# Where the numerator of a rational activation is kept in the first half of a fused attention and two-MoE kernel

## The chip, the core and the metric

The kernel runs on one core of a Trainium2 chip. Its engines are TensorE (PE, with its weight loads shown apart as PEld), VectorE (DVE), ScalarE (ACT), GpSimd (POOL) and SyncE (SP), which only issues transfers. Each engine works through its own queue in order. The metric is the time of one execution on the device in microseconds. Before the change it is 1502.45 us, the median of three runs from 1498.46 to 1506.28.

## What is computed

Three layers in a row: an attention whose keys and values are averaged over groups of eight, a dense layer pair with a rational function between its two products, and a routed layer with eight experts. The change lies in the middle one:

```
h = x @ w_in                                  # 4608 x 512 by 512 x 2048
P = a0 + a1*h + a2*h^2 + a3*h^3
Q = 1 + |b0|*|h| + |b1|*h^2
g = P / (Q + 1e-6)
y = g @ w_out                                 # 2048 x 512
```

The output of the middle layer is routed (each token to one of eight experts by the sorted scores, 576 tokens each) and goes through a two-layer expert. All products are made of rounded parts: an operand is split into a high part and a remainder, and three products (high by high, high by remainder, remainder by high) are summed in PSUM.

## The kernel before

The 4608 tokens are cut into 18 blocks of 256. The 2048 columns of the middle layer are done in two halves of 1024: for all blocks the first half, with its partial outputs stored, then for all blocks the second half. Attention is interleaved with the first half, since it makes the `x` of each block. After the second half come the routing and the experts. In the trace the first half ends at about 596 us, the second at about 1000 us.

A half of a block (or of a pair of blocks) consists of steps. There are 72 steps in each half. A step multiplies `x` by 256 columns of `w_in` (or 128 columns for a pair of blocks) into one PSUM bank `ph` of 128 x 512 numbers (`mm_h`, line L701), and then makes `g` from it:

- `act1`: ACT makes |h| into `ms` (L716), a2 + a3*h into `mw` (L717) and |b0| + |b1|*|h| into `mq` (L719). DVE multiplies `mw` by h (L721), and then makes the numerator without its constant, (mw + a1)*h, which it writes **back into the bank `ph`** (L722). The product `mq*ms` is a `tt` operation (L353), which POOL does.
- `act2`: ACT makes 1/Q in `mr` by a logarithm and an exponential (L734, L736). DVE makes the high part `hi` = (numerator + a0)*`mr` (L737), then `t` = Q*`hi` (L739) and the difference `t` = numerator + a0 - `t` (L741). POOL multiplies it by `mr`, which is the remainder `lo` (L353). `hi` and `lo` together are a buffer `mg` or `mgx`.
- `mm_y`: PE multiplies `hi` by both parts of `w_out` (L805, L806) and `lo` by its high part (L803), into two further banks of 260 columns per 128 tokens, which stay in use over the steps of a block.

In the first half a bank `ph` is thus in use from the step's first matmul to L741. PSUM has eight such banks, named `pa0` to `pa7`. They are shared with the scores (L560), the transposes (L595) and the products (L613 to L616) of attention, and with the preparation of weights (L418 to L422, L440, L444). `mw` and `mq` are rings of three buffers each, taken by the step's number, so a buffer is written again three steps later. `mr` has two and `mt` three.

The order on each engine is not written by hand. Each operation is recorded with its engine, an assumed duration, what it reads and what it writes. A list scheduler then runs through the whole program in its own assumed time: at each point it takes the ready operation with the lowest number on an engine, and an operation that needs a new bank (`Dyn` of `cls_a`) waits until one is free. The instructions are issued in the order that results, and the banks are handed out by it too. The assumed duration of a DVE operation with two tensors depends on its size alone. Before 105 us the scheduler also puts matmuls of zeros on PE (L339) where it expects PE to be idle for 0.4 us or more.

Of the kernel before, what the change touches and what calls it, by code (L numbers as in the profile page):

```python
# [18 lines left out]
ALU = mybir.AluOpType  # L19
# [4 lines left out]
B, H, S, D = 8, 8, 576, 64  # L24
# [7 lines left out]
NB = NT // BLK  # L32
# [97 lines left out]
class Order:  # L130
# [18 lines left out]
    def op(self, eng, dur, fn, r=(), w=(), prio=None, nbytes=0, late=0.0):  # L149
        o = Op()  # L150
        o.alts, o.start, o.late = None, None, late
        o.eng, o.dur, o.fn, o.succ, o.npred, o.ready, o.nbytes = eng, dur, fn, [], 0, 0.0, nbytes
        o.idx = len(self.ops)
        o.prio = o.idx - self.ahead if prio is None else prio
        o.alloc, o.uses, o.bank = [], [], None
        preds = set()
        for k in r:
            p = self.lastw.get(k)
            if p is not None:
                preds.add(p)  # L160
        for k in w:
            p = self.lastw.get(k)
            if p is not None:
                preds.add(p)
            preds.update(self.readers.get(k, ()))
        for k in r:
            self.readers.setdefault(k, []).append(o)
        for k in w:
            self.lastw[k] = o
            self.readers[k] = []  # L170
        for k in {id(x): x for x in (*r, *w)}.values():
            d = k[0] if isinstance(k, tuple) else k
            if isinstance(d, Dyn) and d not in o.uses:
                if d.refs == 0:
                    o.alloc.append(d)
                    o.bank = d
                d.refs += 1
                o.uses.append(d)
        preds.discard(o)
        o.npred = len(preds)  # L180
        for p in preds:
            p.succ.append(o)
        self.ops.append(o)
        return o
# [98 lines left out]
def c_tt(n):  # L283
    return 0.067 + 0.00104 * n


def c_stt(n):
    return 0.06 + 0.00118 * n
# [10 lines left out]
class Kern:  # L299
# [408 lines left out]
    def act1(self, st):  # L708

        nc, op, i = self.nc, self.op, st["i"]  # L710
        ph = st["ph"]
        hk = [(ph, 0)]
        w, q, s = self.mw[i % 3], self.mq[i % 3], self.ms[i % 2]
        st["w"], st["q"] = ph, q
        N = 2 * BLK
        op("Act", c_act(N), lambda: nc.scalar.activation(s(), ph(), AF.Abs), r=hk, w=[s])  # L716
        op("Act", c_act(N, 0, 2), lambda: nc.scalar.activation(w(), ph(), AF.Identity, scale=self.a3(), bias=self.a2()),  # L717
           r=hk + self.sk, w=[w])
        op("Act", c_act(N, 1, 2), lambda: nc.scalar.activation(q(), s(), AF.Identity, scale=self.b1a(), bias=self.b0a()),  # L719
           r=[s] + self.sk, w=[q])  # L720
        op("DVE", c_tt(N), lambda: nc.vector.tensor_tensor(w(), w(), ph(), op=ALU.mult), r=hk, w=[w])  # L721
        op("DVE", c_stt(N), lambda: nc.vector.scalar_tensor_tensor(  # L722
            ph(), w(), self.a1(), ph(), op0=ALU.add, op1=ALU.mult), r=[w], w=hk)
        self.tt(N, q, q, s, ALU.mult, r=[s], w=[q])

    def act2(self, st):

        nc, op, i = self.nc, self.op, st["i"]
        w, q, r, t = st["w"], st["q"], self.mr[i % len(self.mr)], self.mt[i % MTB]
        hi, lo = g = self.mgl.pop(0)  # L730
        self.mgl.append(g)
        st["hi"], st["lo"] = hi, lo
        N = 2 * BLK
        op("Act", c_act(N, 1, 1), lambda: nc.scalar.activation(r(), q(), AF.Ln, scale=2.0 ** -LNS, bias=self.qcs()),  # L734
           r=[q], w=[r])
        op("Act", c_act(N, 1, 1), lambda: nc.scalar.activation(r(), r(), AF.Exp, scale=-1.0, bias=self.nls()), w=[r])  # L736
        op("DVE", c_stt(N), lambda: nc.vector.scalar_tensor_tensor(hi(), w(), self.a0(), r(), op0=ALU.add, op1=ALU.mult),  # L737
           r=[(w, 0), r], w=[hi])
        op("DVE", c_stt(N), lambda: nc.vector.scalar_tensor_tensor(t(), q(), self.qc(), hi(), op0=ALU.add, op1=ALU.mult),  # L739
           r=[q, hi], w=[t])  # L740
        op("DVE", c_stt(N), lambda: nc.vector.scalar_tensor_tensor(  # L741
            t(), w(), self.a0(), t(), op0=ALU.add, op1=ALU.subtract), r=[(w, 0), self.hring(st)], w=[t])
        self.tt(N, lo, t, r, ALU.mult, r=[t, r], w=[lo])

    def late(self, st):
# [755 lines left out]
    def route(self, k):  # L1501

        nc, V, rop = self.nc, self.nc.vector, self.rop
        D = lambda dur, fn, r=(), w=(), late=False: rop("DVE", dur, fn, r=r, w=w, late=late)
        L = lambda dur, fn, r=(), w=(): D(dur, fn, r, w, k > 0)
        tt, ts, stt = V.tensor_tensor, V.tensor_scalar, V.scalar_tensor_tensor
# [9 lines left out]
        q = lambda i: self.q8()[:, i, :]  # L1516
        z = lambda i: self.z1()[:, i:i + 1]
        qk, zk = (lambda i: (self.q8, i)), (lambda i: (self.z1, i))
        K, BQ, ch, M, S2 = self.K, self.BQ, self.ch, self.M if k else self.Mb, self.S2
        cq, cid, ra = self.cq, self.cid, self.ra  # L1520
        rk = lambda x: (self.rp, id(x))
        kk = lambda t, *a: [(t, n) for n in range(*(a or (NB,)))]
        c8 = (ch, 8)
# [28 lines left out]
        def ahead():  # L1552
            cw = lambda t, a, z: t().rearrange("p (g t) -> p g t", t=4)[:, a:z]
            wb = lambda n: self.wrb().unsqueeze(1).unsqueeze(3).to_broadcast([128, n, E, 4])
            for a, z, key in ((0, 8, rk(ch)), (8, 9, c8)):
                if a:
                    D(.1, lambda: ts(ch()[:, 8], self.R()[:, 8], 8.0, None, op0=ALU.is_equal), r=kk(self.R, NB - 2, NB), w=[c8])
                else:
                    D(.34, lambda: V.tensor_reduce(cq()[:, 0:8], K[0]().rearrange("p e g t -> p g t e"), op=ALU.max, axis=AX.X), r=[K[0]], w=[(cq, 0)])
                    own(a, z, key)  # L1560
# [16 lines left out]
        if not last:  # L1577
            if k == 0:
                J, jk = self.small(501, 5)
                D(.07, lambda: V.tensor_copy(J(), self.c("J")), r=[self.rc, *kk(self.R, NB - 2)], w=[jk])  # L1580
                D(.43, lambda: ts(ch()[:, 0:8], self.R()[:, 0:8], 8.0, None, op0=ALU.is_equal), r=kk(self.R, NB - 2), w=[rk(ch)])
                D(.06, lambda: V.memset(self.open8(), 1.0), r=[jk], w=[rk(self.open8)])
            spread(self.kq, BQ)

            def rest():
# [15 lines left out]
              r=[self.rc, (self.thr, 0)], w=[(T, 0), self.rj])  # L1601
            D(.15, lambda: ts(T()[:, E:2 * E], self.c("sel"), so(0)(), None, op0=ALU.mult, op1=ALU.add, accum_out=self.rj()),
              r=[self.rc, (self.sole, 0)], w=[(T, 1), self.rj])
            rop("PE", .2, lambda: nc.tensor.matmul(pt()[:, 0:2 * E], self.c("ones"), T(), start=True, stop=True),
                r=[(T, 0), (T, 1), self.rc], w=[pt])
# [5 lines left out]
              r=[(self.sole, 1), (self.sole, 2)], w=[self.flag])  # L1611
# [5 lines left out]
            def settle():  # L1617
# [4 lines left out]
              w=[rk(M), zk(2), qk(2), K[0], rk(K[1]), K[2], BQ, self.cc, self.chw, (self.chw, 0), (self.chw, 8), self.ge, self.cand, self.nn, self.njunk, self.X, (self.rp, 496), (self.rp, 8), (self.thr, 0), *self.BJ, *[(self.cnt, j) for j in range(4)]])  # L1622
# [361 lines left out]
```

## Time and profile before

| | |
|---|---|
| median of three runs | 1502.45 us (1498.46 to 1506.28) |
| the profiled execution | 1500.95 us, of which the span from the first to the last instruction is 1499.2 us |
| PE busy | 1451.5 us, 97% of the span |
| PEld, DVE, ACT, POOL busy | 87%, 72%, 61%, 58% |
| first half without its first 60 us (60 to 596 us) | PE 518.0, DVE 417.8, ACT 421.2, POOL 361.2 of 536 us |

A busy PE is not PE at its peak, since the ends of matmuls are modelled. But where the profile shows PE idle, time is lost unless PE makes it up from work that is ready, and nothing else in this program is as full as PE. What a stretch has to give is therefore read from PE's idle time in it, from what ended that idle time, and from the granted clock, which falls in some places after PE has been idle. In the list of waits, "PE pa L560 <- DVE mt L741" means that line L560 of PE waited, and that the instruction of line L741 on DVE came last before it went on.

### The profile page before, as it was taken

Reading aid. Unit: us, or ns where it says so; the run is one execution under the profiler, and the core shown is the slowest. Engines: PE = TensorE matmul, PEld = TensorE weight load, DVE = VectorE, ACT = ScalarE, POOL = GpSimd, SP = SyncE. Lnnn points to the kernel's source line nnn. Section 1 sums busy time; section 2 is a strip of 40 time slices with the busy share of each in tenths; the row PEclk is TensorE's granted clock in tenths of the full one; section 3 lists DMA queues with packets and bytes.
Section 4 is the critical chain, followed back from the end, with each engine's and each line's share of the span. In section 5 each row is a group of like instructions: output and inputs, shape, how many; then the busy total and the mean of one; then the engine's idle time right before and its main releaser. Section 6 shows DMA issues by size and latency. Waiting matters only on the chain. (4 is left out here: it accounts for less than half of the span.)

```text
span 1499.2 us, 27379 instructions
## 1 busy us (share of the span) xinstructions
PE 1451.5 (97%) x9516; PEld 1311.2 (87%) x9516; DVE 1077.9 (72%) x2909; ACT 917.9 (61%) x2203; POOL 877.0 (58%) x809
## 2 busy tenths in 40 slices
PE   8899999999999999999999999998999999999998
PEld 7899978888998999888999899766988988988997
DVE  6898787858678587897777877987878877831220
ACT  5887886868778686765446655842554543542431
POOL 5877887557666465764456554842465654653621
PEclk9999999999999999999999999999899999999999
DMA  6672543232422354531343333013254433433400
GB/s 218 221 238 99 168 144 131 80 113 89 144 99 71 103 153 126 166 82 63 111 113 85 85 97 102 1 47 126 86 173 141 152 113 118 155 121 99 140 26 32
DMA packets 109686, 173.62 MB, mean 116 GB/s; under 512 B 10336, under 2 KB 74208, under 8 KB 109536
## 3 DMA queue, kind: packets, MB, share of 16 engines
q1 hardware_dynamic: 84640, 134.02, 27.7%
q0 software_dynamic: 24896, 37.76, 9.1%
q8 instruction: 75, 1.23, 0.3%
q14 instruction: 75, 0.61, 0.1%
HBM read 122.29 MB, written 49.46 MB: 115 GB/s over the span
## 5 line engine op out<-in xcount | busy, mean ns | idle before, releaser
L701 PE MATMUL pa<-xh,wih 128*128 128x256 f32 (+1 forms) x576 | 202.3, 351 | 2.7 <-ACT ex L573 1.2
L701 PE MATMUL pa<-xh,wil 128*128 128x256 f32 (+1 forms) x576 | 195.4, 339 | 0.2 <-POOL wil L353 0.2
L701 PE MATMUL pa<-xl,wih 128*128 128x256 f32 (+1 forms) x576 | 195.2, 339 | 0.0
L353 POOL TENSOR_TENSOR mwq<-mwq,ms 128x512 f32<-128x512 f32 x96 | 130.2, 1357 | 97.4 <-ACT mwq L719 95.9
L716 ACT ACTIVATE ms<-pa 128x512 f32<-128x512 f32 x144 | 85.9, 596 | 113.0 <-PE pa L701 102.0
L1820 PE MATMUL pa<-yth,w1h 128*128 128x256 f32 (+1 forms) x512 | 146.0, 301 | 0.9 <-issue 0.7
L1820 PE MATMUL pa<-ytl,w1h 128*128 128x256 f32 (+1 forms) x512 | 144.9, 299 | 0.0
L1820 PE MATMUL pa<-yth,w1l 128*128 128x256 f32 (+1 forms) x512 | 144.8, 298 | 0.0
L353 POOL TENSOR_TENSOR mg<-mt,mr 128x512 fp32r<-128x512 f32 x75 | 96.9, 1292 | 61.1 <-DVE mt L741 43.2
L805 PE MATMUL pa<-woh,mg 128*128 128x260 f32 x480 | 125.5, 287 | 4.3 <-DVE mg L737 1.9
L806 PE MATMUL pa<-wol,mg 128*128 128x260 f32 x480 | 123.9, 284 | 0.0
L1873 POOL DMA_INDIRECT out<-ob,ix x40 | 39.0, 976 | 144.0 <-ACT ob L1869 116.0
L701 PEld LDWEIGHTS pa<-xh,wih 128*128 128x128 f32 x576 | 109.8, 191 | 14.5 <-ACT ex L573 2.0
L701 PEld LDWEIGHTS pa<-xh,wil 128*128 128x128 f32 x576 | 109.3, 190 | 13.1 <-POOL wil L353 0.4
L701 PEld LDWEIGHTS pa<-xl,wih 128*128 128x128 f32 x576 | 109.7, 190 | 9.1
L573 ACT ACTIVATE ex<-pa,nm 128x72 f32<-128x72 f32 (+2 forms) x320 | 98.6, 326 | 19.8 <-DVE nm L564 14.3
L741 DVE SCALAR_TENSOR_TENSOR mt<-pa,scal,mt 128x512 f32<-128x512 f32 x144 | 106.9, 743 | 1.3
L1823 ACT ACTIVATE h2h<-pa 128x256 fp32r<-128x256 f32 (+1 forms) x128 | 51.0, 407 | 84.9 <-PE pa L1820 79.5
L1854 PE MATMUL pa<-w2h,h2h 128*128 128x512 f32 x256 | 102.7, 401 | 0.0
L1854 PE MATMUL pa<-w2h,h2l 128*128 128x512 f32 x256 | 100.1, 391 | 0.0
L1828 DVE SCALAR_TENSOR_TENSOR h2l<-pa,h2h 128x256 fp32r<-128x256 f32 x128 | 53.7, 419 | 63.9 <-ACT h2h L1823 59.1
L1820 PEld LDWEIGHTS pa<-yth,w1h 128*128 128x128 f32 x512 | 95.9, 192 | 2.1 <-issue 1.5
(438 smaller groups left out, 4942.4 us busy)
## 6 DMA issues: line engine op xcount, KB each, us to landing
mwq<-in_w SPq DMA_DIRECT2D x42, 512.0 KB, 4.4
wraw<-in_w SPq DMA_DIRECT2D x22, 512.0 KB, 5.0
ya_d<-ya SPq DMA_DIRECT2D x18, 520.0 KB, 2.8
yab<-ya_d SPq DMA_DIRECT2D x18, 520.0 KB
kvraw<-in_kT SPq DMA_DIRECT2D x16, 576.0 KB, 4.2
x_d<-xh SPq DMA_DIRECT2D x18, 512.0 KB, 3.9
x_d<-xl SPq DMA_DIRECT2D x18, 512.0 KB
xh<-x_d POOLq DMA_DIRECT2D x18, 512.0 KB
```

The source lines that it names most:

```text
L353: self.g.either({"Pool": (p_tt(n), lambda: nc.gpsimd.tensor_tensor(out(), x(), y(), op=alu)), "DVE": (c_tt(n), lambda: nc.vector.tensor_te ...
L573: op("Act", c_act(NK, 0, 1, 1), lambda h=h: nc.scalar.activation(e()[:n, h, :], sv()[:, h, :], AF.Exp, bias=nm()[:n, h:h + 1], accum_out=s ...
L701: nc.tensor.matmul(o, w()[:, c, f], x()[:, c].rearrange("p b t -> p (b t)") if two else x()[:, c, :], start=c == 0 and k == 0, stop=c == 3 ...
L716: op("Act", c_act(N), lambda: nc.scalar.activation(s(), ph(), AF.Abs), r=hk, w=[s])
L741: op("DVE", c_stt(N), lambda: nc.vector.scalar_tensor_tensor(t(), w(), self.a0(), t(), op0=ALU.add, op1=ALU.subtract), r=[(w, 0), self.hri ...
L805: nc.tensor.matmul(o, hi()[:, f], w(woh), start=first, stop=False)
L806: nc.tensor.matmul(o, hi()[:, f], w(wol), start=False, stop=False)
L1820: nc.tensor.matmul(ps()[:, 0:n], w()[:, c, fs], x()[:, c, :], start=i == 0, stop=i == 11)
L1823: fop("Act", c_act(n), lambda hh=hh, t=t, n=n, ps=ps: nc.scalar.activation(hh()[:, t], ps()[:, 0:n], AF.Relu), r=[ps], w=[(hh, half)])
L1828: fop("DVE", c_stt(t1 - t0), lambda hh=hh, o=o, o0=o0, ps=ps, t0=t0, t1=t1, half=half: nc.vector.scalar_tensor_tensor(o()[:, o0:o0 + t1 - ...
L1854: nc.tensor.matmul(ps(), x()[:, t], w()[:, f % 2, :], start=f == 0 and i == 0, stop=False)
L1873: fop("Pool", 1.05, lambda ob=ob, c=c, n=n: nc.gpsimd.indirect_dma_start(out=self.out, out_offset=bass.IndirectOffsetOnAxis(ap=ix()[:n, c: ...
```

## The change

In the first half L722 writes the numerator into `mw`, its own SBUF input, in place of the bank. The bank `ph` is therefore read last by L722. L737 and the difference (L741 before) read the numerator from `mw`. The product Q*`hi` is written into a fresh PSUM bank `tp` in place of `mt`. The difference reads it there, and writes `mt`. The second half is computed as before. Two further lines add dependencies in the routing, so that operations which write into one bank there keep their order. In the changed kernel the lines of `act2` are called L740 (before L737), L743 (L739) and L745 (L741), and those of `mm_y` L807, L809 and L810 (L803, L805 and L806).

```diff
@@ act1
         op("DVE", c_stt(N), lambda: nc.vector.scalar_tensor_tensor(
-            ph(), w(), self.a1(), ph(), op0=ALU.add, op1=ALU.mult), r=[w], w=hk)
+            (ph if st["half"] else w)(), w(), self.a1(), ph(), op0=ALU.add, op1=ALU.mult),
+           r=[w] if st["half"] else hk, w=hk if st["half"] else [w])
+        if st["half"] == 0:
+            st["w"] = w
@@ act2
         op("DVE", c_stt(N), lambda: nc.vector.scalar_tensor_tensor(hi(), w(), self.a0(), r(), op0=ALU.add, op1=ALU.mult),
-           r=[(w, 0), r], w=[hi])
-        op("DVE", c_stt(N), lambda: nc.vector.scalar_tensor_tensor(t(), q(), self.qc(), hi(), op0=ALU.add, op1=ALU.mult),
-           r=[q, hi], w=[t])
+           r=[(w, 0), w, r], w=[hi])
+        tp = t if st["half"] else Dyn(self.cls_a)
+        op("DVE", c_stt(N), lambda: nc.vector.scalar_tensor_tensor(tp(), q(), self.qc(), hi(), op0=ALU.add, op1=ALU.mult),
+           r=[q, hi], w=[tp])
         op("DVE", c_stt(N), lambda: nc.vector.scalar_tensor_tensor(
-            t(), w(), self.a0(), t(), op0=ALU.add, op1=ALU.subtract), r=[(w, 0), self.hring(st)], w=[t])
+            t(), w(), self.a0(), tp(), op0=ALU.add, op1=ALU.subtract), r=[(w, 0), w, tp, self.hring(st)], w=[t])
@@ route, ahead()
-                    D(.1, lambda: ts(ch()[:, 8], self.R()[:, 8], 8.0, None, op0=ALU.is_equal), r=kk(self.R, NB - 2, NB), w=[c8])
+                    D(.1, lambda: ts(ch()[:, 8], self.R()[:, 8], 8.0, None, op0=ALU.is_equal), r=[(self.rp, 501), *kk(self.R, NB - 2, NB)], w=[c8])
@@ route
-                D(.43, lambda: ts(ch()[:, 0:8], self.R()[:, 0:8], 8.0, None, op0=ALU.is_equal), r=kk(self.R, NB - 2), w=[rk(ch)])
+                D(.43, lambda: ts(ch()[:, 0:8], self.R()[:, 0:8], 8.0, None, op0=ALU.is_equal), r=[jk, *kk(self.R, NB - 2)], w=[rk(ch)])
```

No instruction is added to DVE, ACT or POOL. The rows of PE of the two kernels differ all through the first half. Behind it they are the same apart from the banks they name and from small groups, at the seam between the halves and in the routing, which stand some rows earlier or later. PE's matmuls of zeros (L339) are 212 before and 225 after.

On PE, at about 237 to 243 us of the trace, near the end of block 1's steps (`mg1` and `mg2` are the buffers of two steps, `pa` the banks, `en` the attention weights), before:

```order
L560 MATMUL pa4_231<-kbd0_100,qraw0_102 128x144 x2
L595 MATMUL pa5_233<-ident_115,en2_436 128x128 x3
L803 MATMUL pa3_197<-woh2_1169,mg1_979 128x260
L803 MATMUL pa0_130<-woh2_1169,mg1_979 128x260
L805 MATMUL pa3_197<-woh3_1593,mg2_1159 128x260
...
L805 MATMUL pa1_148<-woh3_1593,mg2_1159 128x260
L806 MATMUL pa1_148<-wol3_1605,mg2_1159 128x260
L701 MATMUL pa6_270<-xh1_795,wih0_145 128x512
```

and in the changed kernel at the same place:

```order
L560 MATMUL pa7_274<-kbd0_100,qraw0_102 128x144 x2
L595 MATMUL pa0_130<-ident_115,en2_436 128x128 x3
L701 MATMUL pa5_233<-xh1_795,wih0_145 128x512
L701 MATMUL pa5_233<-xl1_813,wih0_145 128x512
L701 MATMUL pa5_233<-xh1_795,wil0_191 128x512
L701 MATMUL pa5_233<-xh1_795,wih0_145 128x512
L701 MATMUL pa5_233<-xl1_813,wih0_145 128x512
L701 MATMUL pa5_233<-xh1_795,wil0_191 128x512
L807 MATMUL pa3_197<-woh2_1251,mg1_1080 128x260
```

Six matmuls of a coming step have moved ahead of the products with `lo` of `mg1` (L803, now L807).

On PE, at about 341 to 348 us of the trace, two steps of the same weights `wih2` apart, before (the products with `hi` of `mg0` are the L805 rows, the eight rows of attention's L613 to L616 are cut to the first):

```order
L560 MATMUL pa3_197<-kbd1_112,qraw1_104 128x144 x2
L613 MATMUL pa1_148<-pth0_285,vmh0_120 128x192
...
L803 MATMUL pa4_231<-woh1_628,mg4_1458 128x260
L803 MATMUL pa5_233<-woh1_628,mg4_1458 128x260
L805 MATMUL pa4_231<-woh1_628,mg0_865 128x260
...
L595 MATMUL pa1_148<-ident_115,en2_436 128x128 x3
L701 MATMUL pa0_130<-xh0_353,wih2_976 128x512
```

and in the changed kernel, where the left-out rows ahead of L809 hold eight of attention, two L807, one L595 and nine more L701:

```order
L560 MATMUL pa7_274<-kbd1_112,qraw1_104 128x144 x2
L701 MATMUL pa1_148<-xh0_353,wih2_1014 128x512
L701 MATMUL pa1_148<-xl0_362,wih2_1014 128x512
L701 MATMUL pa1_148<-xh0_353,wil2_1023 128x512
L613 MATMUL pa5_233<-pth0_285,vmh0_120 128x192
...
L809 MATMUL pa0_130<-woh1_628,mg0_873 128x260
```

All twelve matmuls of the next step have moved ahead of the products with `hi` of `mg0`.

On DVE, at one step of the first half (`mg0` is its high part), before:

```order
L737 SCALAR_TENSOR_TENSOR mg0_865<-pa6_270,scal_93,mr1_932 128x512
L627 SCALAR_TENSOR_TENSOR xl1_809<-pa1_148,xh1_795 128x2x192
L739 SCALAR_TENSOR_TENSOR mt2_1193<-mq_1003,scal_93,mg0_865 128x512
L578 TENSOR_SCALAR sm1_214,junk_218<-sm1_214 128x4
L599 TENSOR_TENSOR ptl1_495<-pa2_194,pth1_468 128x2x96
L741 SCALAR_TENSOR_TENSOR mt2_1193<-pa6_270,scal_93,mt2_1193 128x512
```

and in the changed kernel:

```order
L740 SCALAR_TENSOR_TENSOR mg0_873<-mw_943,scal_93,mr1_1049 128x512
L627 SCALAR_TENSOR_TENSOR xl1_813<-pa5_233,xh1_795 128x2x192
L743 SCALAR_TENSOR_TENSOR pa5_233<-mq_954,scal_93,mg0_873 128x512
L578 TENSOR_SCALAR sm1_214,junk_218<-sm1_214 128x4
L599 TENSOR_TENSOR ptl1_495<-pa2_194,pth1_468 128x2x96
L745 SCALAR_TENSOR_TENSOR mt2_1218<-mw_943,scal_93,pa5_233 128x512
```

The order is the same here, and the operands have moved: L740 now reads `mw` and `mr`, which are both in SBUF, L743 writes a bank, and L745 reads one.

## Rows read from the trace of the kernel before

**Rows 1.** The page: the span, and each engine's busy time.
```profile
span 1499.2 us, 27379 instructions
PE 1451.5 (97%) x9516; PEld 1311.2 (87%) x9516; DVE 1077.9 (72%) x2909; ACT 917.9 (61%) x2203; POOL 877.0 (58%) x809
```
**Rows 2.** Stretches: start and end, length, busy time by engine, clock, DMA.
```profile
core 0: us, PE busy (x) PEld busy (x) DVE busy (x) ACT busy (x) POOL busy (x), PEclk, DMA share, GB/s
60.00:596.00 536.00, 517.95 (x3791) 483.67 (x3791) 417.83 (x883) 421.18 (x1212) 361.22 (x398) 0.99 0.40 127
60.00:125.00 65.00, 60.04 (x495) 57.97 (x495) 61.09 (x127) 58.01 (x167) 52.04 (x55) 1.00 0.59 191
...
275.00:300.00 25.00, 23.23 (x139) 19.87 (x138) 22.36 (x47) 21.65 (x56) 14.91 (x17) 1.00 0.17 53
...
400.00:425.00 25.00, 24.47 (x159) 21.89 (x158) 23.10 (x51) 22.65 (x58) 21.31 (x22) 1.00 0.36 114
425.00:596.00 171.00, 170.15 (x1328) 163.19 (x1327) 127.50 (x253) 126.86 (x325) 96.99 (x102) 1.00 0.37 112
```
**Rows 3.** Waits of PE from 60 to 596 us: total, times, longest.
```profile
PE pa L803 <- POOL mg L353: 3.0, 3, 1.6
...
PE pa L805 <- DVE mg L737: 1.9, 2, 1.6
PE pa L560 <- DVE mt L741: 1.9, 3, 0.7
PE pa L805 <- DVE mt L741: 1.4, 2, 0.9
...
PE pa L595 <- DVE mt L741: 0.3, 1, 0.3
```
**Rows 4.** PE in order of time, 233 to 246 us: start, length, instruction, idle before.
```profile
237.29 0.76 PE L560 MATMUL pa<-kbd,qraw 128*128 128x144 f32 x4 [0.47 <-DVE mt L741]
238.64 0.52 PE L595 MATMUL pa<-ident,en 128*128 128x128 f32 x3 [0.59 <-POOL mq L353]
240.74 0.51 PE L803 MATMUL pa<-woh,mg 128*128 128x260 f32 x2 [1.58 <-POOL mg L353]
```
**Rows 5.** PE in order of time, 326 to 349 us.
```profile
328.28 0.40 PE L701 MATMUL pa<-xh,wih 128*128 128x512 f32 x1
328.51 0.39 PE L701 MATMUL pa<-xl,wih 128*128 128x512 f32 x1
...
341.41 0.76 PE L560 MATMUL pa<-kbd,qraw 128*128 128x144 f32 x4 [0.68 <-DVE mt L741]
...
346.58 0.39 PE L805 MATMUL pa<-woh,mg 128*128 128x260 f32 x1 [1.56 <-DVE mg L737]
```
**Rows 6.** PE in two short stretches: busy time, clock granted.
```profile
241.00:244.00 3.00, 3.00 (x14) 0.53 0.13 18
346.00:350.00 4.00, 3.42 (x12) 0.62 0.00 0
```
**Rows 7.** Line L739 alone by stretches: DVE busy (times).
```profile
60.00:596.00 536.00, 73.06 (x70) 0.99 0.40 127
60.00:125.00 65.00, 10.85 (x8) 1.00 0.59 191
```
**Rows 8.** Line L737 alone by stretches.
```profile
60.00:596.00 536.00, 52.12 (x70) 0.99 0.40 127
```
**Rows 9.** Line L739, all of it by form: ns least/median/most, first and last start.
```profile
L739 DVE SCALAR_TENSOR_TENSOR mt<-mwq,scal,mg x57: 740/784/2414, 62.0 to 954.9; 128x512 f32<-128x512 f32 x57
L739 DVE SCALAR_TENSOR_TENSOR mt<-mq,scal,mg x27: 736/851/3358, 85.3 to 948.2; 128x512 f32<-128x512 f32 x27
```
**Rows 10.** Line L741, all of it by form.
```profile
L741 DVE SCALAR_TENSOR_TENSOR mt<-pa,scal,mt x144: 720/742/752, 64.9 to 997.3; 128x512 f32<-128x512 f32 x144
```
**Rows 11.** Groups of DVE, 60 to 596 us: busy, mean ns, idle before, releaser.
```profile
L418 DVE TENSOR_SCALAR pa<-wm 128x512 int32<-128x512 int32 x18 | 12.4, 687 | 0.6 <-ACT wm L417 0.3
```
**Rows 12.** Groups by line: the matmuls of zeros.
```profile
L339 PE MATMUL pa<-idle 128*128 128x256 bf16 x212 | 28.6, 290 | 5.1 <-ACT ex L573 3.1 <-POOL idle L311 1.0 <-DVE xl L627 1.0
```
**Rows 13.** Waits of ACT from 596 to 1000 us.
```profile
ACT mwq L719 <- DVE mt L739: 4.2, 4, 1.5
```

## The prediction

> **What bounds the kernel now.** I read the page first, for the busy shares: PE is busy for 1451.5 of 1499.2 us [rows 1], so nearly the whole time is PE's own work, and a change can only win back PE's idle time or the time PE runs at a lower clock. Then the stretches: from 60 to 596 us, where all but the first steps of the first half lie, PE is idle for 536 - 517.95 = 18.05 us, while DVE is busy for 417.83 us, 78% [rows 2]. That idle time is not spread evenly. From 425 us on PE is full (170.15 of 171 us); in the head, 60 to 125 us, PE is idle for 5.0 us and DVE is busy for 61.09 of 65 us, 94% [rows 2]. So the head leans on DVE, and the end of the half has slack everywhere but on PE. Third, PE's waits in this half, for who ended them: 1.9 + 1.4 + 0.3 = 3.6 us on L741, the last reader of a step's bank, so these are waits for a free bank; 3.0 us on POOL's `lo` and 1.9 us on L737's `hi`, which are waits for data [rows 3]. Last, PE in order of time around the two longest of the data waits. At 237 to 241 us PE waits 0.47 us for a bank, 0.59 us for POOL and then 1.58 us for `lo` [rows 4]; at 341 to 347 us it waits 0.68 us for a bank and then 1.56 us for `hi` [rows 5]. After both its clock is down: 0.53 of full speed from 241 to 244 us and 0.62 from 346 to 350 us [rows 6], about the lower of the two levels, 1.2 GHz, for most of the time.
>
> **The sum** is made against the profiled execution, 1500.95 us: its span of 1499.2 and 1.75 around it. That is 1.5 us under the median of the three runs, which I leave out of the sum.
>
> **Bank released earlier.** The bank `ph` is now free after L722, which stands ahead of L737, L739 and L741 of the same step. The six waits on L741 have that release as their end, so their 3.6 us should go. What comes next in those places is whatever else feeds the same PE row (the queries, the keys, the attention weights), which in the waits shown is smaller; I take 3.0 us, with bounds 0 and 3.6.
>
> **Matmuls moved ahead of the data waits.** An earlier bank lets the scheduler put the next step's matmuls earlier. At the first of the two places six L701 matmuls now stand ahead of the products with `lo`; at the second all twelve of the next step stand ahead of the products with `hi`. One such matmul of 512 columns takes 328.51 - 328.28 = 0.23 us of PE [rows 5], so PE gets 6 x 0.23 = 1.4 us and 12 x 0.23 = 2.8 us of work there, against waits of 1.58 and 1.56 us. That covers 1.4 + 1.56 = 2.96 us. The chain to `hi` and `lo` becomes longer by the price of L740 below, 0.3 us each, so I take 2.4 us, with bounds 0 and 4.9 (both data waits of the half).
>
> **Clock.** If PE is not left idle at those two places, the clock need not fall there. What it costs now is 3.00 x (1 - 0.53) = 1.4 us and 4.00 x (1 - 0.62) = 1.5 us, 2.9 us together [rows 6]. Each place has further idle time ahead of it that may partly stay, so I take 2.2 us, with bounds 0 and 2.9.
>
> **L740 gets a second SBUF input.** L737 reads the numerator from PSUM and `mr` from SBUF, and takes 52.12 / 70 = 0.745 us [rows 8]. L741, also with one input from each, is never over 0.752 us in 144 executions [rows 10]. L739 has the same shape but reads both inputs from SBUF. Its least is the same, 0.74 us, but it reaches 2.4 and 3.4 us [rows 9], and in this stretch it averages 73.06 / 70 = 1.044 us, in the head 10.85 / 8 = 1.356 us [rows 7]. After the change L740 reads `mw` and `mr`, both in SBUF, so its nearest row is L739: + 0.30 us each, + 0.61 us in the head. L743 keeps its two SBUF inputs, and L745 has one, so they stay as they are. Over 72 steps that is 72 x 0.30 = 21.5 us more of DVE.
>
> The Trainium skill, "SBUF — State Buffer", section "Who interferes with whom", gives a reason that speaks against this change: a VectorE instruction with two SBUF inputs contends with a GpSimd instruction that reads SBUF, and the later of the two waits until the other is through. The spread of L739 beside the narrow L741 agrees with it. By this rule the sum carries the 21.5 us of DVE; without it, L740 would be as short as L737, and the forecast would be about 4 us lower.
>
> **How much of it lies on the path.** Of the 536 us DVE is idle for 118 [rows 2], most of it waiting for ACT or PE, and a longer L740 eats from that first. What counts are stretches where DVE is nearly full and PE waits as well: the head, with 8 steps x 0.61 = 4.9 us, and two stretches like 275 to 300 us (DVE 22.36 of 25) and 400 to 425 us (23.10 of 25) [rows 2], with some four steps each, 8 x 0.30 = 2.4 us. Of these 7.3 us I take half, 3.6 us, since PE is still busy for 92% and more there and part of the delay meets work that waits in its queue. Bounds: 0, and 21.5 us if all of it reached PE. The reverse of the contention, POOL held up by L740, adds to an engine that is busy for 361 of 536 us [rows 2]; it is hidden unless `lo` is waited for, and I cost it at nothing.
>
> **The new bank and the longer hold of `mw`.** L743 needs a free bank. If it waits for one, all of DVE's queue waits behind it: L745, the next step's L721 and attention's L564 and L599. The nearest row is L418, which also writes a fresh bank from DVE: 18 executions with 0.6 us idle before them, 0.3 of it for ACT [rows 11], so at most 0.02 us each, 72 x 0.02 = 1.2 us; I take 0.4 us. `mw` is now held until L745, so L717 of the third step after waits for it, and L716 and L719 of that step are in the same queue. `mq`, of the same ring length, is held until L739, one instruction earlier, and its waits are 4.2 us in the whole second half [rows 13]; the first half has fewer steps per microsecond, so nothing. The 13 further matmuls of zeros are 13 x 28.6 / 212 = 1.8 us of PE [rows 12], put where PE is expected to be idle; nothing to 1.8 us, taken as 0.4 us.
>
> **Sum:** 1500.95 - 3.0 - 2.4 - 2.2 + 3.6 + 0.4 + 0.4 = 1497.75 us. The small groups that changed places at the seam and in the routing can go either way by a microsecond or two, and I leave them out. Predicted: 1498 us.
>
> **Rivals.**
> 1. *PE runs ahead.* The two places shown are what happens all through the half: with a bank more, the next step's matmuls are always there when data is late. Then most of the 18.05 us goes, say 13, and the 2.9 us of clock, while L740's price is met by waiting DVE work: 1500.95 - 13 - 2.9 + 2 = 1487 us. For it: both of the longest data waits have such work moved ahead of them. Against it: some of PE's idle time is on attention and loads, which the change does not touch, and the head is DVE's.
> 2. *DVE's longer L740 is the path.* In the stretches where PE waits, it waits for something DVE has yet to do, and DVE gets 21.5 us more to do while the scheduler orders by a duration without it, so rows that were placed to be just ready come late. If two thirds of the 21.5 us reach PE and the gains are 4 us: 1500.95 + 14 - 4 = 1511 us. For it: the head at 94% DVE, and L739's 1.356 us there. Against it: DVE's 118 idle us. From about half of the 21.5 us on, the change is a loss of more than the gains I count.
> 3. *The bank was not what held PE.* The waits are handed to the next late operand, the clock falls elsewhere, and L740 is hidden: 1500.95 - 1 + 2 = 1502 us. For it: 3.6 us of bank waits in 536 us is little. Against it: the two rows of PE that did move.
>
> **How the numbers follow.** The forecast has 0.37, with its own range 1493 to 1504; rival 1 has 0.30, rival 2 0.20, rival 3 0.13. A measurement of this kernel can tell about 0.5%, 7.5 us, from no change: faster means under 1494.9, slower over 1510.0. Rival 1 and the low edge of the forecast give faster 0.36; rival 2 gives slower 0.18, with some of it under the line and a little from rival 3 above it; the rest is 0.46. The range that leaves out 2 in 10 reaches from 1484, just past rival 1, to 1511, rival 2's time.
>
> **What would show it.** Right: no waits of PE on L745 for a bank; clock at or near 1.0 at the two places; L740 spread like L739, mean over 0.95 us, and L745 under 0.76 us; DVE up by about 20 us from 60 to 596 us; PE's idle time there down to about 12 us. Wrong: L740 at 0.75 us (then contention has another cause than the two inputs); DVE idle ahead of L743 that PE or ACT ended (the new bank is waited for); PE's idle time as before or longer in the head (rival 2); or the difference lying behind 1000 us, in the routing.

## The result, and the profile after

The changed kernel takes 1512.05 us, the median of 4 runs from 1511.24 to 1512.48, against 1501.84 us for 4 runs of the kernel before: a ratio of 1.0066, interval 1.0039 to 1.0093. It is slower by 10 us, 0.7%. The forecast was 1498 us, and the range around it reached from 1484 to 1511.

The page of the kernel after, beside [rows 1]: span, then busy time by engine.

```profile
span 1510.0 us, 27387 instructions
PE 1452.6 (96%) x9529; PEld 1307.7 (87%) x9529; DVE 1095.0 (73%) x2909; ACT 917.8 (61%) x2203; POOL 890.1 (59%) x809
```

PE has as much work as before, and the span is 10.8 us longer. So PE idles more. DVE has the same 2909 instructions and is 17.1 us busier, POOL with the same 809 is 13.1 us busier. The store of the first finished rows of the middle layer tells where the time went. Here it stands in the kernel before and then after (start, length, queue, line, operation).

```profile
651.64 0.37 SPq L363 DMA_DIRECT2D y_d<-yb  x1
```

```profile
663.22 0.37 SPq L363 DMA_DIRECT2D y_d<-yb  x1
```

It comes 11.6 us later, which is the whole difference: all is lost by the first block of the second half, and what comes behind it, the routing and the experts included, in sum neither adds nor wins back more than a microsecond. The stretches of the kernel after, columns as in [rows 2]:

```profile
60.00:596.00 536.00, 508.93 (x3696) 470.71 (x3695) 429.00 (x872) 414.81 (x1197) 369.44 (x393) 1.00 0.39 125
425.00:596.00 171.00, 165.29 (x1267) 156.64 (x1266) 134.11 (x250) 125.41 (x318) 101.57 (x102) 1.00 0.34 105
60.00:125.00 65.00, 60.13 (x502) 58.04 (x500) 58.63 (x121) 55.86 (x163) 47.92 (x51) 1.00 0.56 183
```

From 60 to 596 us PE is now idle for 536 - 508.93 = 27.1 us, 9.0 more than in [rows 2]. In the head, where the prediction had put the danger, PE is as busy as before (60.13 us against 60.04), though 5.89 us of it are now matmuls of zeros, against 2.90. With those left out, PE has started 700 matmuls by 125 us where it had started 698, so nothing shows the head to be behind. What was full is not full any more: from 425 us on PE had been idle for 0.85 us and is now idle for 5.7, and from 125 to 200 us for 1.8 and now for 5.1. The second of these stretches, before and then after:

```profile
125.00:200.00 75.00, 73.20 (x577) 69.88 (x577) 57.45 (x133) 63.76 (x207) 58.81 (x69) 1.00 0.49 155
```

```profile
125.00:200.00 75.00, 69.94 (x540) 65.44 (x539) 58.10 (x126) 59.50 (x192) 61.34 (x65) 1.00 0.47 147
```

PE's waits from 60 to 600 us in the kernel after: total, times, longest.

```profile
PE pa L701 <- DVE mt L745: 6.2, 6, 2.0
PE pa L807 <- POOL mg L353: 5.0, 5, 1.9
PE pa L809 <- DVE mg L740: 2.5, 3, 1.6
PE pa L440 <- DVE wf L422: 2.0, 2, 1.9
...
PE pa L339 <- DVE mt L745: 1.1, 2, 0.7
...
PE pa L595 <- DVE mt L745: 1.0, 1, 1.0
PE pa L560 <- DVE mt L745: 0.9, 2, 0.8
...
PE pa L809 <- DVE mt L745: 0.5, 1, 0.5
```

Summed over all rows of this view, PE waits for DVE for 20.0 us, against 7.8 before. The waits on L745, now the last reader of the fresh bank, come to 9.7 us where L741 had 3.6 [rows 3]. They did not go; they grew. Lines L740, L743 and L745 alone, from 60 to 600 us (columns as in [rows 7]):

```profile
60.00:600.00 540.00, 76.11 (x70) 1.00 0.39 125
```

```profile
60.00:600.00 540.00, 67.83 (x69) 1.00 0.39 125
```

```profile
L745 DVE SCALAR_TENSOR_TENSOR mt<-mwq,scal,pa x46: 730/740/749, 64.3 to 591.3; 128x512 f32<-128x512 f32 x46
```

L740 takes 76.11 / 70 = 1.087 us where L737 took 0.745 [rows 8], L743 0.983 us, and L745, with one input from PSUM, stays under 0.75.

The longest L740 is an example of how the price comes about and of where it can go. DVE, POOL and PE of the kernel after in order of time (start, length, instruction, idle before):

```profile
348.79 1.84 POOL L534 TENSOR_TENSOR kvraw<-kvraw 128x768 f32<-128x768 f32 x1
...
350.13 3.24 DVE L740 SCALAR_TENSOR_TENSOR mg<-mw,scal,mr 128x512 fp32r<-128x512 f32 x1
350.60 1.28 POOL L353 TENSOR_TENSOR mwq<-mwq,ms 128x512 f32<-128x512 f32 x1
351.84 0.99 POOL L534 TENSOR_TENSOR kvraw<-kvraw 128x384 f32<-128x384 f32 x1
...
353.43 0.39 PE L809 MATMUL pa<-woh,mg 128*128 128x260 f32 x1 [1.58 <-DVE mg L740]
```

L740 starts while POOL is at work and outlasts three POOL instructions that follow each other without a gap, 3.24 us for work of 0.74; PE then waits 1.58 us for its `hi`.

### The profile page after: what moved, and what is told of

It reads as the page before. It is cut to its first block, busy times and chain, and to the rows that moved or that the text cites. A ratio compares the mean times of both kernels' runs of the same rounds, so it can differ in the third digit from the quotient of the medians.

```text
span 1510.0 us, 27387 instructions
## 1 busy us (share of the span) xinstructions
PE 1452.6 (96%) x9529; PEld 1307.7 (87%) x9529; DVE 1095.0 (73%) x2909; ACT 917.8 (61%) x2203; POOL 890.1 (59%) x809
## 5 line engine op out<-in xcount | busy, mean ns | idle before, releaser
L701 PE MATMUL pa<-xh,wih 128*128 128x256 f32 (+1 forms) x576 | 202.7, 352 | 7.3 <-DVE mt L745 6.2
L701 PE MATMUL pa<-xh,wil 128*128 128x256 f32 (+1 forms) x576 | 195.3, 339 | 0.0
L701 PE MATMUL pa<-xl,wih 128*128 128x256 f32 (+1 forms) x576 | 195.2, 339 | 0.0
L809 PE MATMUL pa<-woh,mg 128*128 128x260 f32 x480 | 125.4, 287 | 5.5 <-DVE mg L740 3.6
L701 PEld LDWEIGHTS pa<-xh,wih 128*128 128x128 f32 x576 | 109.2, 190 | 18.9 <-DVE mt L745 7.7
L810 PE MATMUL pa<-wol,mg 128*128 128x260 f32 x480 | 123.0, 283 | 0.7 <-DVE wol L453 0.7
L701 PEld LDWEIGHTS pa<-xh,wil 128*128 128x128 f32 x576 | 109.2, 190 | 12.9
L701 PEld LDWEIGHTS pa<-xl,wih 128*128 128x128 f32 x576 | 109.4, 190 | 8.7
L353 POOL TENSOR_TENSOR en<-ex,sm 128x256 f32<-128x256 f32 (+5 forms) x160 | 86.5, 562 | 19.6 <-DVE sm L579 12.4
L809 PEld LDWEIGHTS pa<-woh,mg 128*128 128x128 f32 x480 | 90.4, 188 | 8.5 <-DVE mg L740 4.2
```

The lines of the kernel that those rows point to most:

```text
L353: self.g.either({"Pool": (p_tt(n), lambda: nc.gpsimd.tensor_tensor(out(), x(), y(), op=alu)), "DVE": (c_tt(n), lambda: nc.vector.tensor_te ...
L701: nc.tensor.matmul(o, w()[:, c, f], x()[:, c].rearrange("p b t -> p (b t)") if two else x()[:, c, :], start=c == 0 and k == 0, stop=c == 3 ...
L809: nc.tensor.matmul(o, hi()[:, f], w(woh), start=first, stop=False)
L810: nc.tensor.matmul(o, hi()[:, f], w(wol), start=False, stop=False)
```

## The experiments

Each kernel was timed beside the kernel before on the same chip (medians of before 1501.88 to 1502.27 us; ratios are against these). Each expectation says what its theories mean; "the price" is what the second SBUF input of `hi` costs. In the diffs line numbers are left out; where lines were added, `hi` and the subtraction have other numbers, which are given.

**Price without release, first form.** The kernel before, its bank held as before, but `hi` reads `mw` in SBUF, where L721 had left an unfinished numerator.

```
+        v = self.mw[i % 3]
-  hi(), w(), self.a0(), r() ... r=[(w, 0), r]
+  hi(), (w if st["half"] else v)(), self.a0(), r() ... r=[(w, 0), v, r]
```

> The kernel before, except that in the first half the instruction that makes the high part (L737) reads mw from SBUF in place of the bank; the bank is still written by L722 and held to L741 as before. The high part is then made from another operand, and the remainder corrects for it, so the sum of both is nearly the same number. Theory 1 (the price): the second SBUF input makes this instruction longer by about 0.3 us, 72 times, and that reaches PE: 1509 to 1514 us. Theory 2 (the bank): the loss comes from the fresh bank, which PE's next matmuls wait for until L745, and the second SBUF input is hidden: 1500 to 1504 us.

Measured: 1702.21 us, ratio 1.1338 (1.1317 to 1.136). The total says nothing: with these values the routing takes a longer way (28156 instructions, 3697 of DVE instead of 2909). Ahead of the routing the two can be compared: `hi` takes 1.08 us, and the first store of `y_d` starts at 669.38 us, 17.7 later than before. So up to this store the price alone costs more than the whole change does (11.6). Since the total could not be used, it was asked again in another form, further down.

**Release without price.** The kernel after, but ScalarE writes the reciprocal into the fresh bank alone, so `hi` has one SBUF input. GpSimd then finds the logarithm in `mr` and multiplies the remainder by it, so the low part is not the right number here.

```
+        rr = r if st["half"] else tp
-  activation(r(), r(), AF.Exp, ...), w=[r])
+  activation(rr(), r(), AF.Exp, ...), r=[r], w=[rr])
-  hi(), w(), self.a0(), r()
+  hi(), w(), self.a0(), rr()
```

> The changed kernel, except that ACT writes 1/Q of the first half into the fresh bank (from where L740 reads it), which L743 then writes over; so L740 has one SBUF input and the bank of the step is still released at L722. POOL multiplies by the logarithm in place of the reciprocal there, so the remainder part of the product is wrong in the first half. Theory 1 (the price): L740 back at 0.745 us, and the time falls to 1493 to 1501 us. Theory 2 (the bank): the fresh bank is even held longer (from the exponential on), PE still waits some 10 us for L745, 1508 to 1514 us.

Measured: 1495.84 us (1492.91 to 1497.43), ratio 0.9958 (0.9943 to 0.9974), with as many instructions as before on every engine but the zero matmuls of PE. The first `y_d` store is 4.0 us earlier than before. `hi` (L742 there) and the product (L744), each alone:

```profile
60.00:600.00 540.00, 52.60 (x71) 1.00 0.41 128
```

```profile
60.00:600.00 540.00, 67.49 (x71) 1.00 0.41 128
```

They take 0.741 and 0.951 us. So the release does win something, 6.0 us, and what the kernel after has on top of this run, 1512.05 - 1495.84 = 16.2 us, comes with the second SBUF input. (The scheduler's order of instructions differs between these kernels too; a run further down keeps it.) PE's waits for DVE are 7.9 us here against 20.0. The page of this run, its stretch from 60 to 596 us, and its waits on the subtraction (L746 there), the last reader of the fresh bank:

```profile
span 1494.6 us, 27400 instructions
PE 1449.8 (97%) x9523; PEld 1307.2 (87%) x9523; DVE 1068.0 (71%) x2909; ACT 916.9 (61%) x2203; POOL 875.7 (59%) x809
60.00:596.00 536.00, 520.51 (x3836) 485.50 (x3836) 413.35 (x886) 424.39 (x1218) 363.95 (x400) 1.00 0.41 128
PE pa L560 <- DVE mt L746: 1.8, 3, 0.7
PE pa L595 <- DVE mt L746: 1.2, 3, 0.6
PE pa L701 <- DVE mt L746: 1.1, 1, 1.1
```

These waits come to 4.1 us, no less than the 3.6 on L741 before [rows 3]. So the 6.0 us were not won there. PE's idle time fell from 18.05 to 536 - 520.51 = 15.5 us, and the clock of the two places that the prediction named is 1.00 here (from 200 to 250 and from 325 to 350 us), where it was 0.97 and 0.94.

**The scheduler told of the price.** The kernel after, with L740 and L743 planned 0.3 us longer in the first half.

```
+        two = .3 if st["half"] == 0 else 0.0
-  op("DVE", c_stt(N), ... hi() ...   # and the same for the product
+  op("DVE", c_stt(N) + two, ... hi() ...
```

> The changed kernel, with the scheduler told that L740 and L743 take 0.3 us longer in the first half. The instructions are the same, their order and the banks handed out differ. Theory 1 (the price itself is DVE time that PE must wait for): 1508 to 1513 us. Theory 3 (PE's order is planned by durations that are too short, so banks and data come just late): PE's waits on L745, L740 and POOL's remainder shrink from 18 us to under 10, 1499 to 1505 us.

Measured: 1519.79 us, ratio 1.012 (1.0103 to 1.0136). Knowing the mean price does not help; it is 7.7 us worse, and the waits named are 15.2 us, not under 10. But this is no test of the plan alone. In the new order the two instructions are longer still: `hi` (L741 there) averages 80.81 / 68 = 1.188 us and the product (L744) 74.23 / 68 = 1.092, against 1.087 and 0.983. So the run does not show whether a plan made with the wrong duration, part of rival 2's reason, plays a part.

**A third instruction with two SBUF inputs.** The kernel after without the fresh bank: the product goes to `mt`, as before, so the subtraction reads two SBUF tiles too.

```
-        tp = t if st["half"] else Dyn(self.cls_a)
+        tp = t
```

> The changed kernel without the fresh bank: the numerator stays in mw and the product is written into mt as before the change, so L740, L743 and L745 all have two SBUF inputs in the first half. Theory 1 (the price): a third longer instruction, L745 at about 1.05 us as well, 1514 to 1522 us. Theory 2 (the bank): no bank is taken for the product and none is waited for until L745, 1498 to 1505 us.

Measured: 1520.48 us, ratio 1.0127 (1.0111 to 1.0143). All banks are released early and none is taken in addition, and it is 8.4 us slower than the kernel after. L745 now reads:

```profile
L745 DVE SCALAR_TENSOR_TENSOR mt<-mwq,scal,mt x46: 731/752/3146, 63.9 to 592.4; 128x512 f32<-128x512 f32 x46
```

It reaches 3.1 us where with a PSUM input it never passed 0.75. So the fresh bank is not what costs; in sum it saves, since it leaves the subtraction one SBUF input.

**Price without release, second form.** The kernel after, whole computation, but the product goes into the step's own bank, which is thus held to the subtraction as before.

```
-        tp = t if st["half"] else Dyn(self.cls_a)
+        tp = t if st["half"] else st["ph"]
+        tk = t if st["half"] else (tp, 0)
```

(and `tk` for `tp` in the two lists of what is read and written)

> The kernel after, but the product of the first half goes into the step's own bank (the one that the matmuls filled) in place of a fresh one, so that this bank is held to the remainder's subtraction, as before the change, and no second bank is taken; the numerator stays in SBUF, so hi still has two SBUF inputs, and the subtraction one. Theory 1 (the price of hi's second SBUF input reaches TensorE, and the earlier release is what wins something back): the price is 1512.05 - 1495.84 = 16 us, nothing is won back, so 1501.9 + 16 = about 1518, range 1513 to 1523, slower than the kernel after by 2 to 10; hi has a mean of 1.02 to 1.12 us in the first half, the subtraction 0.74; first y_d store 12 to 20 us later than in the kernel before. Theory 2 (price and release belong together: the price is only felt because the early release lets the steps run closer on each other; without it the price hides): 1502 to 1507. Theory 4 (the fresh bank is what costs): without it 1500 to 1505.

Measured: 1520.17 us, ratio 1.0126 (1.0111 to 1.0142); first `y_d` store at 670.65 us, 7.4 later than after. The price is 1520.17 - 1502.03 = 18.1 us without the release and 16.2 with it; the release is worth 6.0 us without the price and 8.1 with it. The two add up, within 2 us; the theory that they belong together falls. The first row of PE's waits (L810 there is a product with `hi`):

```profile
PE pa L810 <- DVE mg L740: 6.0, 5, 4.0
```

This run also settles whether the order of instructions is what costs. From 328.28 us of the kernel before [rows 5] to its first `y_d` store, PE's matmuls and DVE's instructions stand in the same order in both kernels. `hi` averages 74.84 / 68 = 1.101 us, the product 1.072 (1.065 before) and the subtraction 0.739. The matmul of 328.28 us and the store are here at:

```profile
332.59 0.39 PE L701 MATMUL pa<-xh,wih 128*128 128x512 f32 x1
```

```profile
670.65 0.37 SPq L363 DMA_DIRECT2D y_d<-yb  x1
```

The first is 4.3 us late, the second 19.0. So 14.7 us are lost in a stretch where nothing but the length of `hi` has changed noticeably on DVE.

**The reciprocal written twice.** The whole computation, release and no price: ScalarE writes the reciprocal into the fresh bank for `hi`, and again into `mr` for GpSimd.

```
+        rr = r if st["half"] else tp
+        if st["half"] == 0:
+            op("Act", ..., activation(rr(), r(), AF.Exp, ...), r=[r], w=[rr])
         op("Act", ..., activation(r(), r(), AF.Exp, ...), w=[r])
-  hi(), w(), self.a0(), r()
+  hi(), w(), self.a0(), rr()
```

> The kernel after, with the whole computation, but in the first half ScalarE writes the reciprocal twice: first into the fresh bank, from which hi takes it (one SBUF input left), then into SBUF for GpSimd. 72 more activations of about 0.7 us on ScalarE, some 50 us. Theory 1 (what costs is VectorE's second SBUF input beside GpSimd, and a ScalarE operation behind the one that hi waits for delays only the low product): hi at 0.74 us, 1494 to 1502, faster than the kernel after by 10 to 18 and equal to or up to 8 faster than the kernel before. Rival (any longer time of a step's chain reaches TensorE by three quarters, whichever engine it is on): 1495.84 + 0.75 x 50 = about 1533, range 1515 to 1535, with hi at 0.74 all the same.

Measured: 1508.56 us (1506.15 to 1511.44), ratio 1.0046 (1.0031 to 1.0061). Neither expectation hit. `hi` is at 0.744 us, but the first Exp, alone from 60 to 600 us, adds:

```profile
60.00:600.00 540.00, 49.13 (x70) 1.00 0.40 126
```

72 x 49.13 / 70 = 50.5 us of ScalarE cost 1508.56 - 1495.84 = 12.7 us, a quarter. (The profile has DVE busier too, by 1076.0 - 1068.0 = 8.0 us, so not all of it need be ScalarE's.) It is 3.5 us under the kernel after and 6.5 over the kernel before.

**The same in both halves.**

```
-        tp = t if st["half"] else Dyn(self.cls_a)
+        tp = Dyn(self.cls_a)
```

(the numerator to `mw` and the second Exp in both halves as well)

> The run with the reciprocal written twice, and the same in the second half: numerator in SBUF, product and first copy of the reciprocal in a fresh bank, the step's bank free after the numerator. No instruction of VectorE has one SBUF input more than in the kernel before. Theory 1: the second half gains as the first did from the release (6 us there), less what 72 more activations take where ScalarE is busier: 1486 to 1502, hi at 0.74 in both halves. Rival (the second half is not held by banks but by TensorE itself or by the transfers, so there is nothing to win and ScalarE's 50 us more delay the stores and the routing behind): 1500 to 1515.

Measured: 1521.44 us, ratio 1.0124 (1.0109 to 1.014), outside both expectations; the first `y_d` store is where the run before had it (659.07 against 659.32 us), so the 12.9 us more are lost behind it. Whether the second half has nothing to win from the release, or the second Exp eats it, this run does not separate.

**An even delay on DVE, nothing read from SBUF.** The run with release and without price (remainder times the logarithm again, in this and the two runs that follow), and one more DVE instruction ahead of `hi`, bank to bank.

```
+        if st["half"] == 0:
+            op("DVE", .01, ... tensor_scalar(rr()[:, 0:232], rr()[:, 0:232], 1.0, None, op0=ALU.mult), w=[rr])
```

> The run with the release and without the price (release_no_price, its remainder again times the logarithm in place of the reciprocal, 1495.84 us), and in each of the 72 steps of the first half one more VectorE instruction ahead of hi: the first 232 columns of the bank with the reciprocal times 1.0, bank to bank, nothing read from SBUF, so nothing for GpSimd to contend with; some 0.30 us, or 0.40 with the gap to hi behind it. The scheduler isn't told. Theory 1a (VectorE's time in the chain is the price, whatever lengthens it): 72 x 0.30 to 0.40 = 22 to 29 us, of which three quarters reach the end, 16 to 22: 1510 to 1518. Theory 1b (the even 0.3 us would hide as the prediction had it, and what costs is that the contention comes in lumps of up to 2.5 us and lengthens GpSimd's instructions too): 1497 to 1505.

Measured: 1508.33 us (1506.19 to 1512.06), ratio 1.0042 (1.0025 to 1.0058). The instruction, from 60 to 600 us:

```profile
L743 DVE TENSOR_SCALAR pa<-pa 128x232 f32<-128x232 f32 x71 | 28.5, 402 | 22.7 <-ACT pa L741 22.2
```

72 x 0.402 = 28.9 us of DVE cost 12.5 us, 43%. But contention came with it. The pad reads nothing from SBUF; the product (L746 there), which had two SBUF inputs all along, is longer in this run:

```profile
60.00:600.00 540.00, 79.33 (x70) 1.00 0.40 126
```

It averages 79.33 / 70 = 1.133 us, 0.951 without the pad. By the pages DVE is busier by 1107.0 - 1068.0 = 39.0 us, of which 12.5 us are 32%. The forecast of 1510 to 1518 was a little high. The time is outside 1497 to 1505 too, but as the run has contention of its own, it does not rule theory 1b out.

**The same delay behind the subtraction,** on `tp` after L746, where nothing of its own step waits for it.

> The same instruction of VectorE with the same 232 columns, but behind the step's subtraction, on the bank with the product: nothing of its own step waits for it, only what stands behind it on VectorE, and the fresh bank comes free 0.3 us later. If VectorE's time as such is what counts (its queue is on the path wherever it is lengthened): within 3 us of the run with the instruction ahead of hi. If the delay of hi, and with it of the step's chain, is what counts: at most half of that run's loss, 1496 to 1504.

Measured: 1508.97 us (1508.0 to 1510.95), ratio 1.0049 (1.003 to 1.0067), 13.1 us over the run without it, much as ahead of `hi`, with DVE busier by 1092.5 - 1068.0 = 24.5 us. So a loss does not need the step's own `hi` to be late. That DVE's time as such is what counts is not shown, for two reasons. The pad (L750 there) is now the last user of the fresh bank, and PE waits for it; the two largest of six rows are

```profile
PE pa L595 <- DVE pa L750: 2.6, 4, 1.0
PE pa L560 <- DVE pa L750: 2.2, 3, 1.1
```

and all six come to 8.9 us, against 4.1 on the last reader without the pad. And the first `y_d` store is 9.6 us later than without a pad here, but 6.1 us with the pad ahead of `hi`, so some of either loss arises behind the steps that have a pad.

**The same sum in lumps:** every third step alone gets two such instructions, of 232 and of 512 columns.

```
-        if st["half"] == 0:
+        for m in (232, 512) if st["half"] == 0 and i % 3 == 0 else ():
```

> As the run with 232 columns of the bank multiplied by 1.0 ahead of hi in each of the 72 steps (1508.33 us, 0.402 us each, 28.9 us in all), but in every third step alone two such instructions, of 232 and of 512 columns, 0.40 + 0.80 = 1.2 us in 24 steps: the same 29 us of VectorE in lumps, as the contention comes in lumps (18 of 70 hi of the kernel after at 0.75 us, the rest 1.22 in the mean, up to 3.24). If lumps cost more than the even delay, and this is why the price has lost 16.2 us for 27 us of VectorE (60 of 100) and the even pad 12.5 for 28.9 (43 of 100): 1511 to 1515. If the form of the delay does not matter, and the rest of the price lies elsewhere (GpSimd's own instructions, longer beside it): 1506 to 1510.

Measured: 1510.47 us (1509.14 to 1512.92), ratio 1.0051 (1.0031 to 1.0071). They take 0.403 and 0.697 us, 24 x 1.100 = 26.4 us in all, and cost 14.6 us, 55% (half of the 1097.2 - 1068.0 = 29.2 us that DVE is busier). That is just under the first range and just over the second, and the runs of the two pads overlap: whether lumps cost more stays open.

## Why the prediction was wrong

**The step that failed** is "How much of it lies on the path". Of the 21.5 us that L740's second SBUF input adds to DVE it took 3.6 us as reaching PE; the runs show 16.2 to 18.1. With 16.2 for 3.6, and the rest of the sum as it was, the forecast is 1497.75 + 12.6 = 1510.4 us.

The step rested on a reading of DVE's 118 idle us as room that a longer L740 would eat first, so that only stretches with DVE nearly full counted. Neither half of this came out. First, the idle time took less. Beside the run without the price, DVE is busy for 1095.0 - 1068.0 = 27.0 us more; its idle time in the whole span fell from 1494.6 - 1068.0 = 426.6 to 415.0 us, by 11.6, and the span grew by the other 15.4. The prediction had let idle time take 17.9 of 21.5 us, five sixths. Second, the head, DVE's fullest stretch, shows no loss. Against the kernel before, PE's idle time grew by 3.3 us from 125 to 200 us, by 1.0 from 200 to 425 and by 4.9 from 425 to 596, where DVE had been busy for 75 to 77%. And DVE's idle time is mostly a wait for ScalarE: of the 97.2 us of DVE's waits listed for 60 to 596 us in the kernel after, 73.6 end with it. One group of L740, from 60 to 600 us, has 14.8 us of such waits ahead of it, for L739, which in this kernel is ScalarE's exponential (L736 before):

```profile
L740 DVE SCALAR_TENSOR_TENSOR mg<-mwq,scal,mr 128x512 fp32r<-128x512 f32 x34 | 34.1, 1003 | 15.1 <-ACT mr L739 14.8
```

My reading of this, which no run shows directly, is that such a wait is a step of the same loop between PE, ScalarE and DVE; a longer DVE instruction delays the next PE result that ends it, and the wait moves along more than it shrinks. What the pads show is a size: with pads on DVE that read nothing from SBUF, a third to a half of what DVE was busier reached the end (12.5 of 39.0 us, 13.1 of 24.5, 14.6 of 29.2). "Busy for 78%, so there is room" did not hold.

**The price itself was sized well.** L740 rose by 0.34 us over L737, predicted 0.30 (in the head by 0.40, predicted 0.61), and L740 spreads as L739 did. Against the run without the price, the two lines with two SBUF inputs take (1.087 - 0.741) + (0.983 - 0.951) = 0.378 us more in a step, 27.2 us over 72 steps, and 16.2 / 27.2 = 60% of that reaches the end. In the second form of the price without release, which keeps most of the order of the kernel before, it is 18.1 of 1101.5 - 1077.9 = 23.6 us, 77%. That is more than with any pad. What makes the price dearer is not settled: its lumps, or GpSimd's own instructions, which get longer beside it (last section). The prediction had costed these at nothing unless `lo` is waited for. It is: PE's waits on POOL for `lo` are 5.0 us in the largest row, against 3.0 before and 2.9 without the price.

**The gains were right in sum, and not where they were put.** Release, moved matmuls and clock were taken as 3.0 + 2.4 + 2.2 = 7.6 us; the release is worth 6.0 to 8.1. But the first term, 3.0 us for the waits on the last reader of a bank, did not come: these waits are 9.7 us in the kernel after, and 4.1 even without the price, since the fresh bank is held until the subtraction as the step's own bank was. What the rows of the run without the price do show is PE's idle time down by 2.6 us and the clock at 1.00 in both places. In the kernel after one of the clock's two places is better: granted clock and PE from 325 to 350 us, before and after:

```profile
325.00:350.00 25.00, 22.32 (x133) 19.13 (x132) 19.57 (x53) 21.54 (x80) 18.54 (x25) 0.94 0.34 104
```

```profile
325.00:350.00 25.00, 24.15 (x164) 21.57 (x164) 17.22 (x43) 19.63 (x64) 15.67 (x22) 1.00 0.39 125
```

From 200 to 250 us it is 0.97 in both; the drop has moved from 241 to 244 us to between 210 and 220 us (0.83).

**The new bank** was taken as 0.4 us; the run without it is slower, since the bank also spares L745 a second SBUF input. The wait for it is small (DVE's idle time ahead of L743 is 3.5 us over all its groups, part of it ended by L740).

**The rivals.** Rival 2 is what happened: a longer L740 that reaches PE, with gains of 6 instead of 4 us and a price of 16 instead of 14. Its 1511 us is 1 us from the result, which is partly luck, since both sizes were off by 2 us in opposite directions; it had a chance of 0.20. It had leaned on the head, where no loss shows, and its side reason, a plan made without the price, is not shown. Rival 1 does not happen even without the price: that run takes 1495.84 us, not 1487, and PE's idle time falls by 2.6 us, not 13. Rival 3 falls, since the release does win.

## What to carry to other kernels

Before an operand is moved from PSUM to SBUF to release a bank, count which VectorE instructions then read two SBUF tiles while GpSimd is busy, and price each by a neighbour of that kind. Idle time of an engine with an in-order queue is not room: for an engine that stands in a loop with the bounding one, take about half of any added time as reaching the end until a run has measured it (here it was a third to three quarters). A short dummy instruction in the queue gives a first size in one run, without an idea of the mechanism; take the added time from the engine's busy time in the profile, since the pad also changes its neighbours, and ask which buffer it holds longer.

## What the runs showed of the hardware

The contention is sharp. For each line of 128x512 on DVE from 60 to 600 us, the timeline's starts and lengths were sorted by whether a TENSOR_TENSOR of POOL overlaps by more than 0.05 us (count, mean, longest in us):

| kernel, line | inputs from SBUF | alone | beside POOL |
|---|---|---|---|
| after, L740 | 2 | 18, 0.749, 0.75 | 52, 1.220, 3.24 |
| after, L743 (output to PSUM) | 2 | 26, 0.755, 0.76 | 43, 1.121, 2.73 |
| after, L745 | 1 | 31, 0.742, 0.75 | 38, 0.740, 0.75 |
| release without price, `hi` | 1 | 17, 0.746, 0.75 | 54, 0.742, 0.75 |
| third instruction, L745 | 2 | 30, 0.743, 0.76 | 38, 1.205, 3.15 |

The same instruction with one input from PSUM takes no more time beside POOL than alone, and an output in PSUM does not help. POOL pays as well: its 128x512 products take 1.288 us alone (at most 1.33) and 1.434 us beside L740 or L743 (up to 1.85) in the kernel after, 62 of 155 of them against 36 of 158 beside L739 before. The Trainium skill, "SBUF — State Buffer", section "Who interferes with whom", states the rule for two SBUF inputs on VectorE, and these runs agree. It also says that the later of two blocks for the other's whole instruction; L740's 3.24 us beside three POOL instructions in a row is longer than one of these.
